# Attention heads loaded from GpSimd's queue, swaps and row sums ahead on SyncE's, the middle query tile in a slot of its own

## The chip, the cores and the metric

The kernel runs on one core of a Trainium2 chip. The metric is the device time of one execution in microseconds; the median of three runs of the kernel before is 1230.19 us (1230.02 to 1231.67). TensorE (PE) does the matmuls and transposes, VectorE (DVE), ScalarE (ACT) and GpSimd (POOL) the rest, and SyncE (SP) issues transfers. Times are in us from the start of the span.

## The reference: pooled attention, then two feed-forward stages

```python
q_pool = q.reshape(B, H, S // 2, 2, D).mean(axis=3)      # B, H, S, D = 2, 8, 1152, 64
scores = (1 / sqrt(D)) * matmul(q_pool, k^T)
attn = exp(scores - max); attn = attn / (sum(attn) + 1e-9)
x = matmul(attn, v)                                      # -> 1152 tokens x 512
h = x @ w_in; x = (h * tanh(softplus(h))) @ w_out        # 512 -> 2048 -> 512
P = sinkhorn(x @ w_gate)                                 # 8 rounds, 8 experts
out = sum over e of P[:, e] * (relu(x @ w1[e]) @ w2[e])  # 512 -> 1024 -> 512
```

All inputs are float32. The change touches the attention alone, which fills about the first 267 us of the span.

## The kernel before

**Tiles.** A batch has 8 heads, taken two at a time: 8 pairs p. A head has 576 pooled queries, so a pair has 1152, in nine tiles t of 128. Tiles 0 to 3 are the first head's, 5 to 8 the second's, and the middle tile (MID = 4) holds 64 queries of each. Every float32 operand is split into a high and a low part that sit side by side in the contracted dimension (2 x 64 = 128 rows). A step g = 9p + t handles one tile: scores of tile g (L451, into the one score buffer `ps_s`), a copy with the row maximum by VectorE (L466), the exponential by ScalarE (L480), a copy of the result `e` by DMA to a buffer `er` (`hand_over`, L482; two buffers), and, three steps behind, the transposes of `er` (L529), their split (L546, L549) and up to nine matmuls with v (`run_av`, L599).

**Preparation of the heads.** `split_kv` (L355) splits keys or values in two GpSimd operations, part 0 the high and part 1 the low one; `split_q` (L370) takes four steps: sum of the two pooled rows, scale, high, low. `PREP` (L618) gives the tile t at which each is put on GpSimd: `k10` and `k11` are the two parts of the second head's keys of the next pair. `kraw`, `vraw` and `qraw` have one buffer each, so the next load must wait for the last split of the one before. The loads (`load_kv` L333, `load_q` L340) are not issued where the split stands: they are put into the list `loads`, which the main loop empties onto SyncE's queue at the start of the next step (L703). A q load is four DMAs: one per head and one per half of the middle tile.

**Turning.** `trans_k` (L393) transposes keys on TensorE in three parts, `trans_q` (L436) four query tiles at once (u = 0: tiles 0 to 3, u = 1: 4 to 7, u = 2: tile 8), and ScalarE copies them to `qT`. Scores need the high and low rows also with their places exchanged: `swap` (L431), two DMAs from `qT` to itself, again through `loads`. The middle tile gets zero-padded operands `qz` (`middle`, L410) and a swap of its own. `TURN` (L623) gives the tile at which each stands.

**Row sums.** The sums of the exponentials of pair p are inverted and transposed (`turn_sums`, L493), written to DRAM (`out`) and read back, spread over partitions (`back`, three DMAs), both through `loads`; GpSimd multiplies the pair's output with them and splits it (`split_x`, L586). `wgs`, `raw`, `wt`, `wuh`, `wul` belong to weights that are prepared beside the attention.

All transfers of the kernel before are issued by SyncE. A step of the main loop puts its work in this order (shortened):

```python
pre = turn(p, t) if g < NQ else []
waiting, loads[:] = loads[:], []
for f in waiting: f()                 # SyncE: loads, swaps, row sums
scores(g); prep(p, t)                 # prep: GpSimd's splits
if pre: pre.pop(0)()                  # first turning of the step
transposes(g - LAG); hand_over(g - 1) # LAG = 3; hand_over: SyncE
run_av(min(ready, 9))
for f in pre: f()
exps(g)
```

An instruction that has to wait on an engine's queue holds back everything behind it on that queue.

Of the kernel before, what the change touches and what calls it, by code (L numbers as in the profile page):

```python
# [23 lines left out]
def pool_attention_mish_sinkhorn_kernel(  # L24
# [266 lines left out]
    with ExitStack() as actx:  # L291
# [34 lines left out]
        raws, kst, vst, kT, qst, qT = {}, {}, {}, {}, {}, {}  # L326
        loads = []

# [4 lines left out]
        def load_kv(p, j, which, t=None):  # L333
            b, hp, h0 = heads(p)
            t = t or kv_p.tile([P, NK, D], F32, tag=which + "raw", name=f"{which}raw{p}_{j}")
            src = (k if which == "k" else v)[b, h0 + j]
            nc.sync.dma_start(out=t, in_=src.rearrange("(p c) d -> p c d", c=NK))
            raws[which, p, j] = t

        def load_q(p, part=slice(0, QTL)):  # L340
            b, hp, h0 = heads(p)
            if part.start == 0:
                raws["q", p] = q_p.tile([P, QTL, 2, D], F32, tag="qraw", name=f"qraw{p}")
            for j in range(2):
                t0 = j * (MID + 1)
                ts = slice(max(part.start, t0), min(part.stop, t0 + MID))
                if ts.start < ts.stop:
                    src = q[b, h0 + j, 0:2 * MID * P].rearrange("(p t r) d -> p t r d", t=MID, r=2)
                    nc.sync.dma_start(out=raws["q", p][:, ts], in_=src[:, ts.start - t0:ts.stop - t0])
                if part.start <= MID < part.stop:  # L350
                    nc.sync.dma_start(
                        out=raws["q", p][j * D:(j + 1) * D, MID],
                        in_=q[b, h0 + j, 2 * MID * P:S].rearrange("(p r) d -> p r d", r=2))

        def split_kv(p, j, which, eng, part, more=True):  # L355
# [7 lines left out]
            else:  # L363
# [3 lines left out]
                if more and p < NPAIR:  # L367
                    loads.append(lambda: load_kv(p, j, which))

        def split_q(p, eng, step, part=slice(0, QTL)):  # L370
# [17 lines left out]
            if step == 3:  # L388
                split_lo(eng, qst[p][:, part, 1, :], qs, qst[p][:, part, 0, :])
                if part.stop == QTL and p + 1 < NPAIR:  # L390
                    loads.append(lambda: load_q(p + 1))

# [9 lines left out]

        def q_tile(p, t):
            u, i = divmod(t, 4)
            if (p, u) not in qT:
                n = min(4, QTL - 4 * u)
                qT[p, u] = qt_p.tile([P, 2, n, P], F32R, tag=f"qT{n}", name=f"qT{p}_{u}", bufs=2)
            return qT[p, u], i
# [8 lines left out]
        def trans_q0(u):  # L417

            n = min(2, QTL - 2 * u)
            ps = ps_t.tile([P, 2, 2, P], F32R, tag="t", name=f"psq0_{u}")  # L420
            for i in range(n):
                for s in range(2):
                    nc.tensor.transpose(
                        ps[:, i, s, :], qst[0][:, 2 * u + i, s:s + 2, :].rearrange("p a d -> p (a d)"), identr)
            t, i = q_tile(0, 2 * u)
            nc.scalar.activation(
                t[:, :, i:i + n].rearrange("p s n q -> p n s q"), ps[:, 0:n].bitcast(F32), AF.Copy)
            if 2 * u <= MID < 2 * u + n:
                middle(0, ps[:, MID - 2 * u], 2)

# [5 lines left out]
        def trans_q(p, u):  # L436
            ps = ps_t.tile([P, 4, P], F32R, tag="t", name=f"psq{p}_{u}")
            t, _ = q_tile(p, 4 * u)
            n = min(4, QTL - 4 * u)
            for i in range(n):  # L440
                nc.tensor.transpose(
                    ps[:, i, :], qst[p][:, 4 * u + i, 0:2, :].rearrange("p a d -> p (a d)"), identr)
            nc.scalar.activation(t[:, 0], ps[:, 0:n].bitcast(F32), AF.Copy)
            loads.append(lambda: swap(t))
            if 4 * u == MID:
                middle(p, ps, 1)
                loads.append(lambda: swap(qz[p % 2]))

        scS, eS, erS, rsS, rxS = {}, {}, {}, {}, {}

        def scores(g, pl=None):  # L451
            p, t = divmod(g, QTL)
            ps = (pl or ps_s).tile([P, 3, 512], F32, tag="s", name=f"psS{g}")
            for kb in range(3):
                if t == MID:
                    ops = [(qz[p % 2][:, s, j, :], kT[p, j]) for j in range(2) for s in range(2)]
                else:
                    x, i = q_tile(p, t)
                    ops = [(x[:, s, i, :], kT[p, int(t > MID)]) for s in range(2)]
# [33 lines left out]
        def turn_sums(p):  # L493
# [8 lines left out]
            def out():  # L502
                nc.sync.dma_start(out=row, in_=rt)
                loads.append(back)

# [5 lines left out]

            loads.append(out if p == NPAIR - 1 else lambda: loads.append(out))

# [97 lines left out]
        for m in range(1, 2 * NG1 - 1):  # L611
# [6 lines left out]
        PREP = {  # L618
            "q0": 1, "q1": 2, "q2": 3, "q3": 4, "v00": 1, "v01": 2, "v10": 5, "v11": 6,
            "k00": 2, "k01": 3, "k10": 7, "k11": 8,  # L620
        }
        PREP0 = {"k00": 3, "k01": 3, "q0": 4, "q1": 4, "q2": 5, "q3": 5, "v10": 5, "v11": 7, "k10": 7, "k11": 8}
        TURN = {"k0": (5, 6, 7), "k1": (0, 2, 3), "k10": (0, 0, 2), "q0": (2, 2, 3), "q": (6, 1, 2)}  # L623

# [45 lines left out]
        for part in range(4):  # L670
            split_q(0, nc.gpsimd, part, q2)
        def prep(p, t):
            for x, at_ in (PREP if p else PREP0).items():
# [22 lines left out]
        for g in range(T0 + EARLY):  # L696
# [5 lines left out]
            pre = turn(p, t) if g < NQ else []  # L702
            waiting, loads[:] = loads[:], []  # L703
            for f in waiting:
# [607 lines left out]
```

## Time and profile before

| | us |
|---|---|
| median of three runs (lowest, highest) | 1230.19 (1230.02, 1231.67) |
| the profiled execution | 1231.02 |
| its span on the core | 1229.0 |
| TensorE busy, share of the span | 1204.5, 98% |
| VectorE, ScalarE, GpSimd busy | 856.7, 593.8, 623.2 |

The profile is one execution. The span runs from the first to the last record on the core; the execution's own time is 2.0 us longer, for what lies around it. Busy time is the time in which an engine had an instruction in hand; instructions that only issue a DMA aren't counted. A row that says `A <- B` gives a wait of A and what ended it: for TensorE in the attention these are the rows to look for, since its idle time there is the time that a change can win.

### The profile page before, as it was taken

Reading aid. Unit: us, or ns where it says so; the run is one execution under the profiler, and the core shown is the slowest. Engines: PE = TensorE matmul, PEld = TensorE weight load, DVE = VectorE, ACT = ScalarE, POOL = GpSimd, SP = SyncE. Lnnn points to the kernel's source line nnn. Section 1 sums busy time; section 2 is a strip of 40 time slices with the busy share of each in tenths; the row PEclk is TensorE's granted clock in tenths of the full one; section 3 lists DMA queues with packets and bytes.
Section 4 is the critical chain, followed back from the end, with each engine's and each line's share of the span. In section 5 each row is a group of like instructions: output and inputs, shape, how many; then the busy total and the mean of one; then the engine's idle time right before and its main releaser. Section 6 shows DMA issues by size and latency. Waiting matters only on the chain.

```text
span 1229.0 us, 19413 instructions
## 1 busy us (share of the span) xinstructions
PE 1204.5 (98%) x6840; PEld 1113.0 (91%) x6840; DVE 856.7 (70%) x1596; ACT 593.8 (48%) x1364; POOL 623.2 (51%) x704
## 2 busy tenths in 40 slices
PE   8999999999999999999999999999999999999998
PEld 8998888999999999898888889999888899999887
DVE  7898888976444333787866777766866777866865
ACT  7888888977554443552333233333332333333331
POOL 5455566326434332384655565555555565555551
PEclk9999999999999999999999999999999999999999
DMA  6887777653323210011011111111112111111112
GB/s 199 276 277 256 259 251 274 229 192 115 91 69 90 82 31 31 1 52 48 25 40 52 52 43 53 52 52 41 33 39 52 52 43 52 53 52 37 37 39 77
DMA packets 56352, 116.85 MB, mean 95 GB/s; under 512 B 8312, under 2 KB 24896, under 8 KB 56256
## 3 DMA queue, kind: packets, MB, share of 16 engines
q1 hardware_dynamic: 56256, 115.62, 29.3%
q8 instruction: 54, 0.88, 0.3%
q14 instruction: 42, 0.34, 0.1%
HBM read 66.86 MB, written 2.40 MB: 56 GB/s over the span
## 4 chain that ended last, share of the span: by engine, by line
PE 90%; DMA 4%; DVE 3%; ACT 1%; issue 1%; POOL 0%; ACTq 0%; DVEq 0%; POOLq 0%; SPq 0%
PE po L1215 30%; PE c L1045 26%; PE ph L224 10%; PE po L784 8%; PE psS L461 5%; PE psA L564 4%; DMA er<-e 3%; PE psT L543 3%; DVE e L466 2%; DMA qT<-qT 1%; DVE etl L549 1%; PE psk L398 1%; ACT eth L546 0%; ACT e L480 0%; PE psw L629 0%
## 5 line engine op out<-in xcount | busy, mean ns | idle before, releaser
L81 POOL TENSOR_TENSOR wslotsl<-s,wslotsh 128x256 fp32r<-128x256 f32 x180 | 132.4, 744 | 239.2 <-ACT wslotsh L74 239.2
L1223 DVE SCALAR_TENSOR_TENSOR oacc<-po,Pm,oacc 128x512 f32<-128x512 f32 (+1 forms) x217 | 161.2, 747 | 102.9 <-PE po L1215 95.4
L1215 PE MATMUL po<-wdbl,hhall 128*128 128x512 f32 (+1 forms) x543 | 214.4, 395 | 0.0
L1215 PE MATMUL po<-wdbh,hlall 128*128 128x512 f32 (+1 forms) x543 | 214.1, 394 | 0.0
L1215 PE MATMUL po<-wdbh,hhall 128*128 128x512 f32 (+1 forms) x543 | 214.0, 394 | 0.0
L1062 ACT ACTIVATE t<-c 128x384 f32<-128x384 f32 x80 | 39.1, 489 | 248.2 <-PE c L1045 248.2
L1082 ACT ACTIVATE hhall<-c 128x384 fp32r<-128x384 f32 x180 | 88.6, 492 | 128.8 <-DVE c L1078 126.2
L1215 PEld LDWEIGHTS po<-wdbh,hhall 128*128 128x128 f32 x543 | 102.0, 188 | 24.4
L1215 PEld LDWEIGHTS po<-wdbl,hhall 128*128 128x128 f32 x543 | 102.0, 188 | 23.3
L1215 PEld LDWEIGHTS po<-wdbh,hlall 128*128 128x128 f32 x543 | 102.0, 188 | 23.3
L81 POOL TENSOR_TENSOR wslotsl<-rawu,wslotsh 128x256 fp32r<-128x256 f32 x120 | 90.7, 771 | 51.2 <-ACT wslotsh L74 51.2
L466 DVE TENSOR_SCALAR_CACHE_REDUCE e<-psS 128x1152 f32<-128x1152 f32 x72 | 97.3, 1352 | 23.8 <-DMA er<-e 10.5
L549 DVE TENSOR_TENSOR etl<-psT,eth 128x384 fp32r<-128x384 f32 (+1 forms) x240 | 108.0, 507 | 6.2 <-ACT eth L546 6.0
L1083 DVE SCALAR_TENSOR_TENSOR hlall<-c,hhall 128x384 fp32r<-128x384 f32 x180 | 98.7, 549 | 2.1
L546 ACT ACTIVATE eth<-psT 128x384 fp32r<-128x384 f32 (+1 forms) x240 | 92.4, 476 | 9.4 <-PE psT L543 9.1
L1045 PE MATMUL c<-x2h,wslotsl 128*128 128x384 f32 x280 | 94.7, 338 | 0.0
L461 PE MATMUL psS<-kT,qT 128*128 128x384 f32 x384 | 82.5, 347 | 12.5 <-DMA qT<-qT 6.4
L1045 PE MATMUL c<-x2h,wslotsh 128*128 128x384 f32 x280 | 94.4, 337 | 0.0
L1045 PE MATMUL c<-x2l,wslotsh 128*128 128x384 f32 x280 | 94.1, 336 | 0.0
L480 ACT ACTIVATE e<-e,nm 128x1152 f32<-128x1152 f32 x70 | 89.4, 1277 | 0.0
L74 ACT ACTIVATE wslotsh<-s 128x256 fp32r<-128x256 f32 x180 | 72.1, 411 | 24.3 <-DVE s L1011 24.3
L564 PE MATMUL psA<-etl,vst 128*128 128x256 f32 (+1 forms) x288 | 80.4, 303 | 0.5 <-DVE rs L490 0.5
(358 smaller groups left out, 3051.7 us busy)
## 6 DMA issues: line engine op xcount, KB each, us to landing
er<-e SPq DMA_DIRECT2D x70, 576.0 KB, 3.7
rawd<-in_moe_w_dram SPq DMA_DIRECT2D x60, 256.0 KB, 2.9
rawu<-in_moe_w_dram SPq DMA_DIRECT2D x30, 384.0 KB, 3.3
raw<-in_moe_w_in_dram SPq DMA_DIRECT2D x16, 512.0 KB, 4.1
raw<-in_moe_w_out_dram SPq DMA_DIRECT2D x16, 512.0 KB, 3.6
vraw<-in_v_dram SPq DMA_DIRECT2D x16, 288.0 KB, 3.2
kraw<-in_k_dram SPq DMA_DIRECT2D x15, 288.0 KB, 4.3
qraw<-in_q_dram SPq DMA_DIRECT2D x15, 256.0 KB, 6.2
```

The costliest lines, as they stand in the source:

```text
L81: eng.tensor_tensor(out=lo, in0=src, in1=hi.bitcast(F32), op=ALU.subtract)
L224: nc.tensor.matmul(ps[:, 0:TH], lhsT=a, rhs=b, start=(n == 0), stop=(n == len(ops) - 1))
L461: nc.tensor.matmul(ps[:, kb, 0:TH], lhsT=a, rhs=kt[:, kb * TH:(kb + 1) * TH], start=(n == 0), stop=(n == len(ops) - 1))
L466: nc.vector.tensor_scalar(sc, ps[:, :, 0:TH], -1.0, None, op0=ALU.mult, op1=ALU.min, accum_out=nm)
L546: nc.scalar.activation(eh[:, cs, o:o + b - a], ps[:, 0:3, a:b], AF.Copy)
L549: nc.vector.tensor_tensor(out=el[:, cs, o:o + b - a], in0=ps[:, 0:3, a:b], in1=eh[:, cs, o:o + b - a].bitcast(F32), op=ALU.subtract)
L564: nc.tensor.matmul(box["ps"][:, 0:n], lhsT=vst[p, j][:, c].rearrange("p a d -> p (a d)"), rhs=(el, eh)[which][:, c, 0:n], start=(c == 0 an ...
L784: nc.tensor.matmul(ps[:, 0:TH], lhsT=a, rhs=b, start=(n == 0), stop=(n == len(ops) - 1))
L1045: nc.tensor.matmul(cb[c], lhsT=a_, rhs=b_, start=FIRST[n] and m == 0, stop=LAST[n] and m == len(ops) - 1, skip_group_check=True)
L1083: los.append(lambda: nc.vector.scalar_tensor_tensor(out=lo, in0=b, scalar=0.0, in1=hi.bitcast(F32), op0=ALU.max, op1=ALU.subtract))
L1215: nc.tensor.matmul(ps[:, 0:w], lhsT=a, rhs=b[:, cs], start=(n == 0), stop=(n == len(ops) - 1))
L1223: nc.vector.scalar_tensor_tensor(out=oa, in0=ps[:, 0:w], scalar=gate, in1=oa, op0=ALU.mult, op1=ALU.add)
```

## The change

Loads of keys, values and queries of the main loop are issued on GpSimd's queue, right where the last split of their buffer stands, in place of SyncE's queue one step later (`loader`). Those of the start, before the main loop, stay on SyncE. A q load is one DMA for both heads and two for the middle tile. Swaps and row sums go into a list `first`, which is emptied ahead of `loads`; the row sums' `out` no longer waits a step more. In `qst` and `qraw` the middle tile takes the last slot (8), and tiles 5 to 8 take slots 4 to 7, so `qT` is two groups of four tiles, the middle tile is turned alone (u = 2) at t = 0 of its pair where u = 2 stood at t = 2, and the swap of a one-tile group is gone. `v11` moves from t = 6 to t = 5.

```diff
--- before.py
+++ after.py
@@ -324,7 +324,8 @@
             qz.append(t)
 
         raws, kst, vst, kT, qst, qT = {}, {}, {}, {}, {}, {}
-        loads = []
+        loader = nc.sync
+        loads, first = [], []
 
         def heads(p):
             b, hp = divmod(p, HPB)
@@ -334,22 +335,24 @@
             b, hp, h0 = heads(p)
             t = t or kv_p.tile([P, NK, D], F32, tag=which + "raw", name=f"{which}raw{p}_{j}")
             src = (k if which == "k" else v)[b, h0 + j]
-            nc.sync.dma_start(out=t, in_=src.rearrange("(p c) d -> p c d", c=NK))
+            loader.dma_start(out=t, in_=src.rearrange("(p c) d -> p c d", c=NK))
             raws[which, p, j] = t
 
         def load_q(p, part=slice(0, QTL)):
             b, hp, h0 = heads(p)
             if part.start == 0:
                 raws["q", p] = q_p.tile([P, QTL, 2, D], F32, tag="qraw", name=f"qraw{p}")
-            for j in range(2):
-                t0 = j * (MID + 1)
-                ts = slice(max(part.start, t0), min(part.stop, t0 + MID))
-                if ts.start < ts.stop:
-                    src = q[b, h0 + j, 0:2 * MID * P].rearrange("(p t r) d -> p t r d", t=MID, r=2)
-                    nc.sync.dma_start(out=raws["q", p][:, ts], in_=src[:, ts.start - t0:ts.stop - t0])
-                if part.start <= MID < part.stop:
-                    nc.sync.dma_start(
-                        out=raws["q", p][j * D:(j + 1) * D, MID],
+            src = q[b, h0:h0 + 2, 0:2 * MID * P].rearrange("h (p t r) d -> p h t (r d)", t=MID, r=2)
+            dst = raws["q", p][:, 0:2 * MID].rearrange("p (h t) r d -> p h t (r d)", h=2)
+            if part.stop - part.start == QTL:
+                loader.dma_start(out=dst, in_=src)
+            else:
+                h, ts = (0, part) if part.stop <= MID else (1, slice(0, MID))
+                loader.dma_start(out=dst[:, h, ts], in_=src[:, h, ts])
+            if part.stop == QTL:
+                for j in range(2):
+                    loader.dma_start(
+                        out=raws["q", p][j * D:(j + 1) * D, 2 * MID],
                         in_=q[b, h0 + j, 2 * MID * P:S].rearrange("(p r) d -> p r d", r=2))
 
         def split_kv(p, j, which, eng, part, more=True):
@@ -365,7 +368,7 @@
                 split_lo(eng, t[:, :, 1, :], raw, t[:, :, 0, :])
                 p, j = (p, 1) if j == 0 else (p + 1, 0)
                 if more and p < NPAIR:
-                    loads.append(lambda: load_kv(p, j, which))
+                    load_kv(p, j, which)
 
         def split_q(p, eng, step, part=slice(0, QTL)):
             if p == NPAIR:
@@ -388,7 +391,7 @@
             if step == 3:
                 split_lo(eng, qst[p][:, part, 1, :], qs, qst[p][:, part, 0, :])
                 if part.stop == QTL and p + 1 < NPAIR:
-                    loads.append(lambda: load_q(p + 1))
+                    load_q(p + 1)
 
         def trans_k(p, j, c3):
             if c3 == 0:
@@ -400,11 +403,14 @@
                 kT[p, j][:, c3 * TH:(c3 + 1) * TH],
                 ps[:, 0:3, :].bitcast(F32).rearrange("p a d -> p (a d)"), AF.Copy)
 
-        def q_tile(p, t):
-            u, i = divmod(t, 4)
+        def slot(t):
+
+            return t if t < MID else t - 1 if t > MID else 2 * MID
+
+        def q_tile(p, x):
+            u, i = divmod(x, MID)
             if (p, u) not in qT:
-                n = min(4, QTL - 4 * u)
-                qT[p, u] = qt_p.tile([P, 2, n, P], F32R, tag=f"qT{n}", name=f"qT{p}_{u}", bufs=2)
+                qT[p, u] = qt_p.tile([P, 2, MID, P], F32R, tag="qT", name=f"qT{p}_{u}", bufs=2)
             return qT[p, u], i
 
         def middle(p, ps, n):
@@ -422,11 +428,12 @@
                 for s in range(2):
                     nc.tensor.transpose(
                         ps[:, i, s, :], qst[0][:, 2 * u + i, s:s + 2, :].rearrange("p a d -> p (a d)"), identr)
+            if 2 * u == 2 * MID:
+                middle(0, ps[:, 0], 2)
+                return
             t, i = q_tile(0, 2 * u)
             nc.scalar.activation(
                 t[:, :, i:i + n].rearrange("p s n q -> p n s q"), ps[:, 0:n].bitcast(F32), AF.Copy)
-            if 2 * u <= MID < 2 * u + n:
-                middle(0, ps[:, MID - 2 * u], 2)
 
         def swap(t):
 
@@ -435,16 +442,17 @@
 
         def trans_q(p, u):
             ps = ps_t.tile([P, 4, P], F32R, tag="t", name=f"psq{p}_{u}")
-            t, _ = q_tile(p, 4 * u)
-            n = min(4, QTL - 4 * u)
+            n = min(MID, QTL - MID * u)
             for i in range(n):
                 nc.tensor.transpose(
-                    ps[:, i, :], qst[p][:, 4 * u + i, 0:2, :].rearrange("p a d -> p (a d)"), identr)
-            nc.scalar.activation(t[:, 0], ps[:, 0:n].bitcast(F32), AF.Copy)
-            loads.append(lambda: swap(t))
-            if 4 * u == MID:
+                    ps[:, i, :], qst[p][:, MID * u + i, 0:2, :].rearrange("p a d -> p (a d)"), identr)
+            if u == 2:
                 middle(p, ps, 1)
-                loads.append(lambda: swap(qz[p % 2]))
+                t = qz[p % 2]
+            else:
+                t, _ = q_tile(p, MID * u)
+                nc.scalar.activation(t[:, 0], ps[:, 0:n].bitcast(F32), AF.Copy)
+            first.append(lambda: swap(t))
 
         scS, eS, erS, rsS, rxS = {}, {}, {}, {}, {}
 
@@ -455,7 +463,7 @@
                 if t == MID:
                     ops = [(qz[p % 2][:, s, j, :], kT[p, j]) for j in range(2) for s in range(2)]
                 else:
-                    x, i = q_tile(p, t)
+                    x, i = q_tile(p, slot(t))
                     ops = [(x[:, s, i, :], kT[p, int(t > MID)]) for s in range(2)]
                 for n, (a, kt) in enumerate(ops):
                     nc.tensor.matmul(
@@ -501,7 +509,7 @@
 
             def out():
                 nc.sync.dma_start(out=row, in_=rt)
-                loads.append(back)
+                first.append(back)
 
             def back():
                 flat = row.rearrange("t p -> (t p)")
@@ -509,7 +517,7 @@
                     nc.sync.dma_start(
                         out=rx[j * D:(j + 1) * D, x:x + n], in_=flat[a:a + n].unsqueeze(0).to_broadcast([D, n]))
 
-            loads.append(out if p == NPAIR - 1 else lambda: loads.append(out))
+            first.append(out)
 
 
         c0, c1 = 2 * P, SQ
@@ -616,11 +624,11 @@
 
 
         PREP = {
-            "q0": 1, "q1": 2, "q2": 3, "q3": 4, "v00": 1, "v01": 2, "v10": 5, "v11": 6,
-            "k00": 2, "k01": 3, "k10": 7, "k11": 8,
+            "q0": 1, "q1": 2, "q2": 3, "q3": 4, "v00": 1, "v01": 2, "k00": 2, "k01": 3,
+            "v10": 5, "v11": 5, "k10": 7, "k11": 8,
         }
         PREP0 = {"k00": 3, "k01": 3, "q0": 4, "q1": 4, "q2": 5, "q3": 5, "v10": 5, "v11": 7, "k10": 7, "k11": 8}
-        TURN = {"k0": (5, 6, 7), "k1": (0, 2, 3), "k10": (0, 0, 2), "q0": (2, 2, 3), "q": (6, 1, 2)}
+        TURN = {"k0": (5, 6, 7), "k1": (0, 2, 3), "k10": (0, 0, 2), "q0": (2, 2, 3), "q": (6, 1, 0)}
 
 
 
@@ -669,6 +677,8 @@
         scores(1, ps_b)
         for part in range(4):
             split_q(0, nc.gpsimd, part, q2)
+        loader = nc.gpsimd
+
         def prep(p, t):
             for x, at_ in (PREP if p else PREP0).items():
                 if at_ == t:
@@ -700,7 +710,8 @@
                 ps_t = pool("ps_t", 4, space=PSUM)
                 ps_a = pool("ps_a", 1, space=PSUM)
             pre = turn(p, t) if g < NQ else []
-            waiting, loads[:] = loads[:], []
+            waiting = first + loads
+            first[:], loads[:] = [], []
             for f in waiting:
                 f()
             if g < LAG:
```

## Rows read from the trace of the kernel before

**Rows 1.** Busy time by stretch: us, then PE, PEld, DVE, ACT, POOL busy (instructions), PEclk, DMA share, GB/s
```profile
99.60:132.00 32.40, 30.41 (x241) 29.42 (x242) 29.28 (x60) 28.08 (x64) 19.11 (x20) 1.00 0.77 266
...
264.00:400.00 136.00, 135.86 (x788) 135.79 (x789) 65.58 (x121) 78.22 (x155) 57.49 (x44) 1.00 0.34 98
400.00:1229.00 829.00, 823.38 (x4145) 741.65 (x4144) 559.99 (x999) 288.12 (x698) 427.31 (x517) 1.00 0.15 45
...
48.00:232.00 184.00, 170.75 (x1347) 164.17 (x1345) 163.17 (x333) 159.51 (x360) 105.94 (x102) 1.00 0.77 263
```

**Rows 2.** Waits of PE, 48 to 232 us: total us, times, longest us
```profile
PE psS L461 <- DMA qT<-qT: 6.4, 6, 1.9
PE psT L543 <- DMA er<-e: 3.4, 6, 1.3
PE psS L461 <- DVE e L466: 2.9, 6, 0.5
```

**Rows 3.** Timeline of pair 3: start us, us, engine, line, operation, tiles [idle before <- releaser]
```profile
118.48 0.42 DVE L581 TENSOR_TENSOR xs<-psA,avt 64x256 f32<-64x256 f32 x1
...
124.36 0.60 ACT L443 ACTIVATE qT<-psq 128x512 fp32r<-128x512 f32 x1
...
125.90 0.92 PE L543 MATMUL psT<-identr,er 128*128 128x128 f32 x9 [0.42 <-DMA er<-e]
...
127.31 1.32 PE L461 MATMUL psS<-kT,qT 128*128 128x384 f32 x6 [0.48 <-DVE e L466]
...
132.02 1.12 PE L461 MATMUL psS<-kT,qT 128*128 128x384 f32 x5 [1.10 <-DMA qT<-qT]
...
132.97 0.37 PE L398 MATMUL psk<-identr,kst 128*128 128x128 f32 x3
```

**Rows 4.** SyncE's queue in pair 3, same columns (us: while the issues held the queue)
```profile
113.70 2.15 SPq L509 DMA_DIRECT2D rx<-row  x3
...
117.17 0.54 SPq L349 DMA_DIRECT2D qraw<-in_q_dram  x1
...
119.40 0.51 SPq L351 DMA_DIRECT2D qraw<-in_q_dram  x1
120.01 3.27 SPq L486 DMA_DIRECT2D er<-e  x2
127.06 0.33 SPq L337 DMA_DIRECT2D vraw<-in_v_dram  x1
127.44 1.12 SPq L434 DMA_DIRECT2D qT<-qT  x2
```

**Rows 5.** Waits of SyncE's queue, 0 to 268 us: total us, times, longest us
```profile
SPq L337 <- POOL vst L81: 20.6, 7, 3.8
```

**Rows 6.** Chain of work that ended last, pair 3: start us, us, what
```profile
120.01 5.76 DMA er<-e
127.98 3.91 DMA qT<-qT
```

**Rows 7.** DMA to landing: that of `er`, 30 to 265 us; key loads of the whole span (count, KB, us)
```profile
DMA to landing us min/median/max: 3.0/3.7/5.8
...
kraw<-in_k_dram SPq DMA_DIRECT2D x15, 288.0 KB, 4.3
```

**Rows 8.** Issue of key loads on SyncE's queue, 30 to 265 us: ns min/median/max
```profile
L337 SPq DMA_DIRECT2D kraw<-in_k_dram x12: 334/530/702, 33.3 to 215.4; - x12
```

**Rows 9.** GpSimd in pair 3, columns as in rows 3
```profile
110.49 0.68 POOL L78 TENSOR_SCALAR qst<-qraw 128x576 fp32r<-128x576 f32 x1 [6.81 <-PE psq L441]
...
112.53 1.44 POOL L81 TENSOR_TENSOR qst<-qraw,qst 128x576 fp32r<-128x576 f32 x1
120.01 1.44 POOL L590 TENSOR_TENSOR xs<-xs,rx 128x576 f32<-128x576 f32 x1 [6.04 <-DMA rx<-row]
...
130.09 1.44 POOL L81 TENSOR_TENSOR kst<-kraw,kst 128x576 fp32r<-128x576 f32 x1
```

**Rows 10.** ScalarE and PE in pair 0, columns as in rows 3
```profile
15.81 0.45 ACT L414 ACTIVATE qz<-psq 128x128 fp32r<-128x128 f32 x2
...
16.87 1.31 ACT L546 ACTIVATE eth<-psT 128x384 fp32r<-128x384 f32 x3
...
17.11 2.35 PE L461 MATMUL psS<-kT,qz 128*128 128x384 f32 x12
```

## The prediction

> **What bounds the kernel now.** The busy time by stretch comes first. After the attention TensorE has no gap that a change here could use: 135.86 of 136 us, then 823.38 of 829 us [rows 1]. In the attention it has. From 48 to 232 us, pairs 1 to 6, it is busy 170.75 of 184.0 us, so 13.2 us are idle; VectorE with 163.2 and ScalarE with 159.5 us stand close behind, GpSimd with 105.9 does not [rows 1].
>
> The waits of TensorE name that time: 6.4 us for `qT<-qT`, the swaps; 3.4 us for `er<-e`, the copies handed over; 2.9 us for VectorE's copy `e` [rows 2]. Together 12.7 of the 13.2 us. The third follows from the second: `e` writes a buffer that a late `er` copy has to read first.
>
> The timeline of pair 3 shows one period. TensorE waits 0.42 us for `er` at 125.90, 0.48 us for `e` at 127.31, 1.10 us for the swap at 132.02: 2.0 us in 32.4 [rows 3, 1].
>
> SyncE's queue shows why. ScalarE has written `qT` at 124.36 + 0.60 = 124.96 [rows 3], but its swap is issued at 127.44, behind a value load at 127.06 [rows 4]. That load waits for GpSimd's split of its buffer; such waits held the queue for 20.6 us in seven cases, up to 3.8 us [rows 5]. The swap's chain then ends 3.91 us after 127.98, at 131.89 [rows 6]. For `er` it is the q load: its DMAs go out from 117.17, the last at 119.40, the `er` copy at 120.01 behind them [rows 4], and that copy takes 5.76 us where the median is 3.7 [rows 6, 7].
>
> **The change, part by part.**
>
> *Loads off SyncE's queue.* Per full pair SyncE loses 4 issues for keys and values and 4 for q, with all waits for GpSimd's splits. The swap can then go out at about 125.0 in place of 127.44, and land 2.4 us earlier, at 129.5. TensorE stood ready for it at 132.02 - 1.10 = 130.92, and will at 130.0 when the 0.9 us of the two earlier waits are gone. Margin 0.5 us, so the 6.4 us go. The `er` copy no longer follows a q load: issued about as before, it needs its usual 3.7 us and not 5.76, so 2.1 us more are at hand than the 0.42 us that lacked. Then the 3.4 and, with them, the 2.9 us go. Sum of waits removed: 12.7 us.
>
> *Loads on GpSimd's queue.* Pairs 1 to 5 get seven issues each: two of keys, two of values, three of q; pairs 0 and 6 get some of them. No row shows an issue on GpSimd. Lower bound: SyncE's shortest issue of a key load, 0.33 us [rows 8]. Upper bound: an issue that held GpSimd until the data landed, 4.3 us [rows 7]. I take 1.0 us, between SyncE's median of 0.53 us for this same load [rows 8] and GpSimd's own two-input operation on a tile of that size, 1.44 us [rows 9]: the same work, done by that engine. [...]
>
> GpSimd's share: 19.1 us busy per pair [rows 1] + 7 x 1.0 = 26.1 in some 31, so it isn't the bound as a whole. But one stretch is tight. It starts with `xs` (the product with the row sums) at 120.01 and ends with `k11`, at 130.09 + 1.44 = 131.53 [rows 9]: 11.5 us with no gap. `k11` feeds `psk` of the next pair's t = 0, at 132.97 [rows 3], where TensorE would now be 2.0 us earlier, at 130.97. `xs` waited for `rx` (6.04 us idle [rows 9]). The change writes the row sums one step (32.4 / 9 = 3.6 us) earlier, so `rx`, issued at 113.70 [rows 4], lands near 116.4 in place of 120.0 and no longer sets it: VectorE's last piece of `xs`, ready at 118.48 + 0.42 = 118.90 [rows 3], does. So `xs` starts at 119.0, and `k11` ends at 119.0 + 11.5 + 1.0 for the v load now in the stretch = 131.5. TensorE waits 0.5 us. Pairs 2, 3 and 4 hold the same weight work there; pair 5 lacks one 0.7 us operation and comes out even. Price: 3 x 0.5 = 1.5 us. At 0.33 us an issue it is 0, at 4.3 us it is 3.8 us a pair and more.
>
> Behind `k11` on GpSimd stand the next load and the next pair's q steps; these have room. In the kernel before, the high part of q waits 6.81 us for `psq` of u = 2 [rows 9]; now the last group is u = 1, one step earlier, and the loads of k and q that follow go out earlier too. If that cover fails, `xs` starts later and `k11` with it, one for one.
>
> *Middle tile.* One swap (two issues) and one ScalarE copy less per pair; the two `qz` copies move from t = 1 to t = 0, four steps ahead of use. In pair 0 the middle tile is turned at t = 3, one step ahead of use. Its two copies (0.45 us [rows 10]) come in front of the first `eth` copies, as before, since the first turning of a step precedes the transposes. The `eth` of that step began at 16.87 and the scores on `qz` at 17.11 [rows 10]. I cost it at 0, between -0.3 (a copy less) and +0.45 us. The early `v11` precedes `k11` either way: 0.
>
> *What is late next.* Loads now leave in a burst behind GpSimd's splits and still pass through the same DMA engines, which are 77% busy [rows 1]; VectorE, with 163.2 us of work against 170.75 of TensorE's, leaves little room to catch up. I put back 0.42 us per pair, pair 3's wait for `er` [rows 3], for six pairs: 2.5 us. Bounds: 0, and 6.3 us where both `er` terms stay whole.
>
> **Sum.** 12.7 - 1.5 - 2.5 = 8.7 us off. The profiled execution's own 1231.0 becomes 1222.3; it lies 0.8 us above the median of the runs, so I forecast 1221.5. Behind the attention nothing swallows the gain: TensorE is full there, and the weights' loads are tied to the same steps, so they move along.
>
> [...] The `er` copy took 5.76 us right behind a q load and 3.7 in the median [rows 6, 7], while one queue carried both. [...]
>
> **The rivals.**
>
> 1. *The copies are as late as before*, since q loads and `er` share the engines. For it: the 77%. Against it: loads move to other moments, ahead of t = 4. The swaps' 6.4 us are won, the 6.3 us of `er` and `e` are not, and `k11` costs its 1.5: 4.9 us, 1225.3. Chance 0.15.
> 2. *All waits go and an issue on GpSimd is cheap* (0.33 us): 12.7 us, 1217.5. Chance 0.15.
> 3. *GpSimd becomes the bound* (slower). Its work per pair is 19.1 + 7c, with c the cost of an issue; the period is 32.4. It decides from c = (32.4 - 19.1) / 7 = 1.9 us. At 2.2 us the pair takes 34.5, 2.1 us more, over five pairs 10.5 us: 1240.7. [...] Against it: 2.2 us is four times SyncE's median issue. Chance 0.15.
> 4. *Even*: at about 1.9 us per issue gain and loss cancel, 1230. Chance 0.09.
>
> That the loads stay where they are isn't a rival: they are plain calls on another queue, and SyncE keeps only weights, swaps, row sums and `er`.
>
> **How the numbers follow.** Forecast 0.46, rivals 0.15, 0.15, 0.15 and 0.09. A difference of 0.2% (2.5 us) is about what a measurement of this kernel can tell from no change. Faster by over 0.2%: 0.46 + 0.15 + 0.15 = 0.76; within: 0.09; slower: 0.15. The low end, 1216.5, is rival 2 less 1 us for ScalarE's lighter load. The high end, 1234, takes in rivals 1 and 4 and the start of rival 3 (c = 2.0 gives 0.7 us a pair, 3.5 in all); what lies above, 0.14, and below, 0.05, is left out.
>
> **What would show it.** Right: `PE psS <- DMA qT` gone from the waits of TensorE, `er` and `e` below 2.5 us in all; swaps on SyncE within 0.2 us of ScalarE's `qT`; a new wait `PE psk <- POOL kst` of about 0.5 us in pairs 2 to 4; a pair near 31.3 us (32.4 - 2.0 + 0.5 + 0.4). Wrong: gaps of 2 us or more on GpSimd around its DMA issues, a period above 32.4 us with `psk` waiting for `kst`; or waits for `er` of the old size; or waits for weights after 264 us that give the gain back.

## The result, and the profile after

The changed kernel takes 1242.78 us in the median (1239.69 to 1242.97, four runs) against 1230.18 of the kernel before on the same chip (four runs): ratio 1.0092, 95% interval 1.0076 to 1.0108. The medians are 12.6 us apart, and the spans of the two profiled executions 11.5 us. The forecast of 1221.5 us, faster, was wrong in sign. The profiled execution took 1242.97 us, its span is 1240.5.

The four largest waits of TensorE from 48 to 232 us in the kernel after (total us, times, longest us), which answer to [rows 2]:

```profile
PE psq L447 <- DVE etl L557: 7.4, 4, 1.9
PE psS L469 <- DVE e L474: 5.9, 9, 0.9
PE psr L504 <- DVE rs L499: 1.4, 3, 0.5
PE psk L401 <- POOL kst L81: 1.2, 3, 0.4
```

Neither `qT` nor `er` stands there any more. The DMA waits of [rows 2] are gone, and VectorE has taken their place. From the timeline of pair 3 in the kernel after, VectorE, GpSimd and TensorE around t = 0 (start us, us, engine, line, operation):

```profile
95.97 1.36 DVE L474 TENSOR_SCALAR_CACHE_REDUCE e<-psS 128x1152 f32<-128x1152 f32 x1
96.56 0.60 POOL L338 DMA_DIRECT2D kraw<-in_k_dram  x1 [0.30 <-POOL kst L81]
97.18 1.43 POOL L379 TENSOR_TENSOR qraw<-qraw 128x576 f32<-128x576 f32 x1
97.25 4.17 DVE L156 TENSOR_SCALAR wt<-raw 128x256 uint32<-128x256 uint32 x1
98.57 0.68 POOL L78 TENSOR_SCALAR vst<-vraw 128x576 fp32r<-128x576 f32 x1
99.22 0.68 POOL L381 TENSOR_SCALAR qraw<-qraw 128x576 f32<-128x576 f32 x1
99.85 1.40 POOL L81 TENSOR_TENSOR vst<-vraw,vst 128x576 fp32r<-128x576 f32 x1
101.34 1.48 DVE L557 TENSOR_TENSOR etl<-psT,eth 128x384 fp32r<-128x384 f32 x3
101.55 0.58 POOL L338 DMA_DIRECT2D vraw<-in_v_dram  x1 [0.30 <-POOL vst L81]
101.94 0.53 PE L447 MATMUL psq<-identr,qst 128*128 128x128 f32 x4 [1.85 <-DVE etl L557]
102.17 0.69 POOL L78 TENSOR_SCALAR kst<-kraw 128x576 fp32r<-128x576 f32 x1
103.13 1.79 DVE L498 TENSOR_SCALAR rs<-rs 128x9 f32<-128x9 f32 x1
103.45 1.43 POOL L81 TENSOR_TENSOR kst<-kraw,kst 128x576 fp32r<-128x576 f32 x1
```

VectorE's shift of a weight piece (L156) begins at 97.25, just after GpSimd began a run of four splits with no gap between them. It ends at 101.42, right behind the end of the last one, 99.85 + 1.40 = 101.25, and ahead of the next DMA issue. The same happens to the add on nine row sums (L498): it ends at 104.92, behind the split that ends at 103.45 + 1.43 = 104.88. Behind L156 wait `etl`, and for `etl` TensorE, 1.85 us.

The same place of pair 3 in the kernel before:

```profile
101.29 1.45 POOL L81 TENSOR_TENSOR vst<-vraw,vst 128x576 fp32r<-128x576 f32 x1
102.21 0.68 DVE L156 TENSOR_SCALAR wt<-raw 128x256 uint32<-128x256 uint32 x1
103.00 0.68 POOL L78 TENSOR_SCALAR kst<-kraw 128x576 fp32r<-128x576 f32 x1 [0.27 <-DMA kraw<-in_k_dram]
104.60 0.15 DVE L490 TENSOR_SCALAR rs<-rs 128x9 f32<-128x9 f32 x1
```

There L156 starts 0.53 us before GpSimd's splits come to a pause (101.29 + 1.45 = 102.74) and ends 0.15 us behind that, and the add on the row sums stands while GpSimd is idle.

VectorE's groups from 60 to 250 us, kept apart by shape (xcount | busy us, mean ns | idle before). Kernel before:

```profile
L162 DVE SCALAR_TENSOR_TENSOR wt<-raw,wt 128x256 uint32<-128x256 uint32 x12 | 9.7, 809 | 0.0
L156 DVE TENSOR_SCALAR wt<-raw 128x256 uint32<-128x256 uint32 x12 | 5.8, 485 | 0.0
L490 DVE TENSOR_SCALAR rs<-rs 128x9 f32<-128x9 f32 x6 | 0.9, 153 | 0.0
```

Kernel after, the same operations:

```profile
L156 DVE TENSOR_SCALAR wt<-raw 128x256 uint32<-128x256 uint32 x12 | 20.0, 1670 | 0.0
L498 DVE TENSOR_SCALAR rs<-rs 128x9 f32<-128x9 f32 x6 | 7.8, 1296 | 0.0
L162 DVE SCALAR_TENSOR_TENSOR wt<-raw,wt 128x256 uint32<-128x256 uint32 x11 | 7.6, 691 | 0.0
```

The work is the same, but for one L162 that falls behind 250 us in the kernel after, and takes 35.4 us in place of 16.4. L162 is not part of the rise: its mean is 809 ns before and 691 after. The other part of the loss is TensorE's clock. Busy time of 2 us windows in the kernel after (PE, PEld, DVE, ACT, POOL; then PEclk, DMA share, GB/s):

```profile
106.00:108.00 2.00, 1.32 (x6) 1.00 (x6) 2.00 (x5) 1.35 (x2) 1.70 (x2) 1.00 0.93 272
108.00:110.00 2.00, 1.97 (x13) 1.83 (x14) 2.00 (x4) 1.34 (x3) 1.29 (x3) 0.56 0.55 54
110.00:112.00 2.00, 2.00 (x9) 2.00 (x10) 1.97 (x6) 0.49 (x2) 0.00 (x0) 0.59 1.02 384
112.00:114.00 2.00, 2.00 (x20) 1.96 (x19) 1.24 (x3) 1.71 (x4) 0.00 (x0) 1.00 0.42 165
```

Between 100 and 108 us TensorE was busy for 0.15, 2.00, 1.11 and 1.32 us of the four windows of 2 us, at a granted clock of 1.00. Behind that the granted clock is 0.56 and 0.59 of full speed from 108 to 112 us, though TensorE is busy again. The same comes in pair 4 (0.50 at 146 us) and pair 6 (0.51 at 214 us, 0.50 at 216 us), not in pair 5 (1.00 from 182 to 186 us). Over the span TensorE is busy 1212.8 us against 1204.5 before, 8.3 us more for the same 6840 matmuls, and idle 27.7 against 24.5, 3.2 us more; together the 11.5 us by which the span grew. In wt_later below, with the stalls gone, the granted clock is 1.00 from 0 to 267 us, and TensorE's first 1956 matmuls take 252.05 us of busy time, as in the kernel before (252.16), against 260.4 in the kernel after.

Time between the starts of two score copies `e` on VectorE's timeline, pair 3 (us; the last step runs to the next pair's t = 0):

| kernel | t = 0 to 1 | 1 to 4 | 4 to 8 | 8 to 0 | pair |
|---|---|---|---|---|---|
| before | 3.99 | 10.77 | 13.07 | 4.66 | 32.49 |
| after | 9.11 | 12.38 | 12.96 | 2.77 | 37.22 |
| best2 | 4.24 | 11.22 | 16.82 | 2.90 | 35.18 |
| gap | 3.61 | 11.14 | 18.31 | 3.16 | 36.22 |
| q_on_sync | 4.17 | 11.23 | 13.59 | 2.78 | 31.77 |

The rows are of the profiled executions. That of q_on_sync, 1223.8 us, is close to its median, but best2's took 1230.64 and gap's 1242.58 us, 4.4 and 6.1 us above theirs. The gain forecast is there where the swap's wait was, from t = 8 to 0. It is lost, more than twice over, in the step behind it.

### The profile page after: what moved, and what is told of

Read it like the earlier page. It is cut to its first block, busy times and chain, and to the rows that moved or that the text cites. A ratio compares the mean times of both kernels' runs of the same rounds, so it can differ in the third digit from the quotient of the medians.

```text
span 1240.5 us, 19363 instructions
## 1 busy us (share of the span) xinstructions
PE 1212.8 (98%) x6840; PEld 1117.6 (90%) x6840; DVE 875.2 (71%) x1596; ACT 593.2 (48%) x1356; POOL 651.4 (53%) x750
## 4 chain that ended last, share of the span: by engine, by line
PE 90%; DVE 7%; issue 2%; ACT 1%; POOL 0%; ACTq 0%; POOLq 0%; DVEq 0%
PE po L1226 30%; PE c L1056 25%; PE ph L224 10%; PE po L795 8%; PE psS L469 5%; PE psA L572 5%; PE psT L551 3%; DVE etl L557 2%; DVE e L474 2%; DVE wt L156 1%; PE psk L401 1%; DVE rs L498 1%; PE psw L637 0%; PE pg L850 0%; DVE wt L162 0%
```

## The experiments

The theory (H in the texts on record): a run of GpSimd's splits without a gap holds VectorE's operations that read and write SBUF alone until it ends, and the change makes these operations start early in such runs. Its rivals put the loss on the transfers that GpSimd issues, or on VectorE as a full engine.

### The held operations moved: wt_later, sums_in_psum, both

wt_later moves the four weight operations of VectorE, which stood at t = 0 to 3, to t = 3 and 4:

```diff
-                at(ts[1] + 2 * j, "dve", lambda cs=cs: shift(cs))
-                at(ts[1] + 2 * j + parts - 1, "dve", lambda cs=cs: sign(cs))
+                w = ts[1] + j if parts > 1 else ts[1]
+                at(w, "dve", lambda cs=cs: shift(cs))
+                at(w, "dve", lambda cs=cs: sign(cs))
...
-        load_w(0, 0, [(t, t + 2, t + 7, t + 8, t + 9) for t in evenly(16, 9)], 2, parts=2, busy=True)
+        load_w(0, 0, [(t, t + 5, t + 7, t + 8, t + 9) for t in evenly(16, 9)], 2, parts=2, busy=True)
...
```

The next line, for the second weight, changes alike. sums_in_psum leaves the weights and does the row sums' add and reciprocal behind their transpose, on PSUM; both has the two edits.

```diff
-            nc.vector.tensor_scalar(rs, rs, EPS, None, op0=ALU.add)
-            nc.vector.reciprocal(rs, rs)
...
-            nc.vector.tensor_copy(rt, ps[0:QTL, 0, :])
+            nc.vector.tensor_scalar(ps[0:QTL, 0, :], ps[0:QTL, 0, :], EPS, None, op0=ALU.add)
+            nc.vector.reciprocal(rt, ps[0:QTL, 0, :])
```

> Theory H (held): a VectorE operation with all its operands in SBUF gets no start while GpSimd runs without a gap. In the changed kernel the weight operations of VectorE (wt, L156) stood 1.67 us in the mean where 0.28 us is their least, 16.6 us too much over 60 to 250 us. Here they move to t = 3 and t = 4 of a pair, where GpSimd stands idle behind its loads. H expects wt at 0.28 us again, most of 16 us back: 1226 to 1231 us, while rs still stands 1.8 us. Theory G (GpSimd is the bound, by its seven DMA issues of 0.6 to 0.7 us and a 0.3 us wait each): nothing moves by more than 2 us, 1241 to 1244 us.

> Only the row sums' two small VectorE operations change: they are done behind the transpose, with PSUM as their source, and no longer on the SBUF tile rs (1.30 us in the mean where 0.15 is the least, 6.9 us too much over six pairs). H expects the new operations at 0.3 us or less each, and 4 to 8 us back: 1235 to 1239 us, with wt still held for about 4 us. G: no change, 1241 to 1244 us.

> Both moves in one kernel. H: VectorE is free of holds, the waits that the change removed stay removed, TensorE's clock has no reason to fall: 1217 to 1222 us, below the kernel before. G: 1240 us or more.

Measured: wt_later 1227.59 us (ratio 0.9977, 0.9966 to 0.9989): the whole loss and 2.6 us more come back, though every load is still issued on GpSimd, and L156 takes 290 ns in the mean. sums_in_psum 1239.46 (1.0071, 1.0056 to 1.0086) is 0.5 us above its range. both 1227.4 (0.9974, 0.996 to 0.9988) is 5.4 us above its range and no better than wt_later. The replacement is dear itself: VectorE's groups of L156 in wt_later and of the new reciprocal in both, 946 ns for nine rows:

```profile
L156 DVE TENSOR_SCALAR wt<-raw 128x256 uint32<-128x256 uint32 x12 | 3.5, 290 | 0.0
...
L506 DVE RECIPROCAL rt<-psr 9x128 f32<-9x128 f32 x6 | 5.7, 946 | 0.2
```

So the weight operations carry most of the loss.

### One held operation put back: best, probe_add, probe_reciprocal

best is wt_later with the add of the row sums on ScalarE. The probes add to it one useless operation of nine elements at t = 0, its result unused:

```diff
...
-            nc.vector.tensor_scalar(rs, rs, EPS, None, op0=ALU.add)
+            nc.scalar.activation(rs, rs, AF.Copy, bias=EPS)
...
+                if p and t == 0 and g < NQ:
+                    nc.vector.tensor_scalar(probe, ones[:, 0:9], 1.0, None, op0=ALU.add)
```

In probe_reciprocal the last line is `nc.vector.reciprocal(probe, ones[:, 0:9])`.

> The changed kernel with VectorE's weight operations at t = 3 and t = 4, and the 1e-9 added to the row sums by ScalarE; the reciprocal stays on VectorE, since it took 0.215 us in every run, held or not. H: rs is gone from the held operations, the step t = 0 to t = 1 shrinks from 5.5 us (weights moved alone) to about 4.1, with the next step at 2.85: 1.4 us in each of four to five pairs less than the 1227.6 of the weights moved alone: 1220 to 1224 us. Rival S (what is left is set by VectorE's own work and TensorE, and the hold of rs lies beside other work): 1226 to 1229 us.

> As the kernel called best, with one useless VectorE operation in step t = 0 of each pair from 1 to 7, behind the copy of the scores: 9 elements per partition, SBUF to SBUF, an add. Its result is not used. H: it is held until GpSimd's run has its next gap, 2 to 4 us in pairs 2 to 5, and the kernel gets slower than best by 6 us or more. Rival (VectorE's long weight operations were slow by their own size, 256 elements with a stride of two): 0.06 to 0.2 us an operation and at most 1 us in all.

> The same useless operation at the same place and of the same size, but a reciprocal. If every SBUF operation of VectorE is held by GpSimd's run, it stands 2 to 4 us too and the time is that of probe_add. If only some forms are held, as the steady 0.215 us of the reciprocal behind rs suggests, it stands 0.22 us and the kernel is within 2 us of best.

best 1227.88 (0.9976, 0.9963 to 0.999) missed its 1220 to 1224 and came out in its rival's range; VectorE now waits for ScalarE's add, 7.1 us in six times. probe_add 1236.41 (1.0056, 1.0035 to 1.0078), probe_reciprocal 1230.05 (0.9996, 0.9984 to 1.0008). VectorE's group of the probe in probe_add, and the probe of pair 3 in the timeline beside GpSimd's last split of that run:

```profile
L734 DVE TENSOR_SCALAR probe<-ones 128x9 f32<-128x9 f32 x6 | 12.1, 2016 | 0.0
...
100.87 4.07 DVE L734 TENSOR_SCALAR probe<-ones 128x9 f32<-128x9 f32 x1
103.50 1.40 POOL L82 TENSOR_TENSOR vst<-vraw,vst 128x576 fp32r<-128x576 f32 x1
```

The same group in probe_reciprocal:

```profile
L734 DVE RECIPROCAL probe<-ones 128x9 f32<-128x9 f32 x6 | 1.3, 209 | 0.0
```

An add of nine elements, 0.17 us in pairs 1, 2 and 7, takes 4.07 us until GpSimd's run ends at 104.90; in pairs 4 to 6 it takes 3.95, 1.24 and 2.50 us. The seven cost the kernel 8.5 us against best and 6.4 against probe_reciprocal. A reciprocal of the same size in the same place is not held: its seven took 0.21 us each, and its kernel is 2.2 us slower than best, close to the 2 us set. At the same size and place one kind is held and the other is not: that tells the theory from a VectorE that is merely full, and narrows it to some kinds of operation.

### Gaps opened in GpSimd's run: gap

The changed kernel, with two tiny GpSimd operations a pair that read VectorE's results, so that GpSimd stands still while VectorE works:

```diff
...
+                if parts == 2 and cs.start == 0:
+                    x = box["t"][:, 0:1].bitcast(I32)
+                    nc.gpsimd.tensor_tensor(out=mark_i, in0=x, in1=x, op=ALU.add)
...
+            if p < NPAIR - 1:
+                nc.gpsimd.tensor_scalar(mark_f, rs, 1.0, 0.0, op0=ALU.mult, op1=ALU.add)
```

> The changed kernel with every operation of VectorE where the change left it. Added are two tiny GpSimd operations per pair that read what VectorE wrote: one element per partition of wt behind the first weight operation of a chunk (t = 0), and the nine row sums behind their reciprocal. GpSimd must wait for VectorE there, so its run gets a gap exactly where VectorE needs one; it has 6 to 11 us to spare later in the pair. H: wt at t = 0 and rs fall to 0.3 and 0.15 us, the step t = 0 to t = 1 from 9.1 to about 4.5 us, 4 us or more in each of pairs 3 to 6: 1222 to 1229 us. If the operations are slow for their own place or size, or GpSimd's work is what bounds: 1240 us or more, since GpSimd only gets more to do.

1236.47 us (1.0048, 1.0029 to 1.0066), 7.5 us above its range and 3.5 below the rival's. The timeline of pair 3 shows that the hold itself is gone:

```profile
105.06 0.29 DVE L158 TENSOR_SCALAR wt<-raw 128x256 uint32<-128x256 uint32 x1
105.44 0.18 POOL L163 TENSOR_TENSOR mark_i<-wt 128x1 int32<-128x1 int32 x1 [4.42 <-DVE wt L158]
107.08 0.15 DVE L503 TENSOR_SCALAR rs<-rs 128x9 f32<-128x9 f32 x1
107.65 0.21 POOL L506 TENSOR_SCALAR mark_f<-rs 128x9 f32<-128x9 f32 x1 [2.02 <-DVE rs L504]
```

0.29 us in place of 4.17 (in all of pairs 2 to 6), and t = 0 to 1 takes 3.61 us in place of 9.11 (table above): the expected effect in its place. But GpSimd stands idle for 4.42 and 2.02 us, its next value load goes out 8.6 us behind the `e` copy of t = 0 in place of 5.6, and from t = 4 to 8 the pair loses 5 us. The waits of TensorE from 48 to 232 us name `er`; that the later loads make it late was not tried by itself:

```profile
PE psT L558 <- DMA er<-e: 13.8, 6, 3.2
```

### Where the loads are issued: loads_on_sync, before_moved, loads_alone, sync_moved

loads_on_sync puts all loads of the changed kernel back through the list (`loads.append(lambda: load_kv(p, j, which))`, the same for q); sync_moved has that and the moves of best2 below. loads_alone is the kernel before with nothing but its loads issued by GpSimd right behind their splits. before_moved is the kernel before with the moves of best.

> The changed kernel with its loads back on SyncE's queue, through the list as in the kernel before; the early middle tile, the order of swaps and row sums and the merged q load stay. G (the issues on GpSimd are what costs): back to 1230 us or below. H (GpSimd's gapless run holds VectorE, with or without DMA issues in it): rs and wt are still held for 1.5 us or more each, 1232 us or more.

> The kernel before with the same two moves and nothing of the change. In it wt stood 0.48 us and its second operation 0.81 us in the mean, together 7 us above their least over six pairs, partly under waits for DMA. H: 0 to 5 us faster than before, 1225 to 1230 us, with the waits for the swaps and for er whole: slower than best by 3 us or more. If best is no faster than this one, the change itself gives nothing.

> The kernel before with one part of the change alone: keys, values and queries loaded from GpSimd's queue behind its splits. Middle tile, swaps, row sums and v11 as before. H: the waits of TensorE for the swaps and er fall to 3 us or less, the pair's boundary comes earlier, so wt at t = 0 starts earlier in GpSimd's run and is held 3 to 4 us; rs falls into the gap in which GpSimd waits for the last query turning and stays at 0.15 us: 1231 to 1238 us, between the two kernels. If the loads were good by themselves and the middle tile did the harm: 1224 us or less.

> The changed kernel with loads back on SyncE and the same two moves as best2. It tells what GpSimd's queue is worth once nothing is held: the waits for er (8.5 us in loads_on_sync) should stay, the rest as in best2: 3 to 6 us slower than best2. If it is as fast, the loads' move is worth nothing by itself.

loads_on_sync took 1230.1 (1.0001, 0.9982 to 1.002), where the theory had wanted a loss and holds of 1.5 us or more. Its rival's time was right. What speaks against the rival is wt_later, which keeps every issue on GpSimd and takes 1227.59 us, and the timeline gives a cause that fits the theory:

```profile
99.15 1.44 POOL L81 TENSOR_TENSOR vst<-vraw,vst 128x576 fp32r<-128x576 f32 x1
100.06 0.68 DVE L156 TENSOR_SCALAR wt<-raw 128x256 uint32<-128x256 uint32 x1
100.99 0.67 POOL L78 TENSOR_SCALAR kst<-kraw 128x576 fp32r<-128x576 f32 x1 [0.40 <-DMA kraw<-in_k_dram]
```

GpSimd's run, with no issue in it, ends at 99.15 + 1.44 = 100.59. L156 starts 0.53 us before that end and ends 0.15 us behind it, at 100.74, in the 0.40 us wait for a load. What L156 paid was the rest of the run that it started in: 0.68 us with 0.53 us left here, 4.17 us with 4.0 us left in the changed kernel. before_moved 1230.77 (1.0005, 0.9995 to 1.0015) is 0.8 us above its range and 2.9 us above best: the moves by themselves win nothing in the kernel before. It isn't a kernel without holds, though. GpSimd is busy where L156 now stands: it takes 726 ns in the mean against 485, and the reciprocal waits 5.1 us for ScalarE.

loads_alone 1247.91 (1.0147, 1.0131 to 1.0163) was slower than either theory had it. From its chain of waits in pair 3 (start us, us, what):

```profile
122.91 8.53 DMA er<-e
131.44 0.14 issue
131.57 1.36 PE psT L544 x9
```

An `er` copy takes 8.53 us there, beside a q load that GpSimd issued from 121.39 to 123.57 and a weight load of 512 KB that SyncE issued at 119.25; TensorE waits 14.6 us for `er` in five times. On one queue the longest copy had taken 5.8 us [rows 7]. Which of the two loads makes the copy late isn't shown by this kernel. sync_moved 1232.51 (1.002, 1.0008 to 1.0032) is 6.3 us above best2, where 3 to 6 were set: with L156 at 0.29 us in both, all loads on GpSimd are worth that much against all on SyncE. Its wait for `er` is 4.7 us, not the 8.5 expected.

### What is left of the forecast: best2, q_on_sync, q_in_halves

best2 is wt_later with the add of the row sums on ScalarE at the end of t = 8, where nothing waits for it:

```diff
                 if g < NQ:
                     exps(g)
+                    if t == QTL - 1:
+                        nc.scalar.activation(rsS[p], rsS[p], AF.Copy, bias=EPS)
```

q_on_sync is best2 with the q load alone back on SyncE, one step later (`loads.append(lambda: load_q(p + 1))`, `nc.sync` in `load_q`). q_in_halves keeps it on GpSimd and issues the second head's half and the middle tile two steps later.

> As best, but ScalarE adds the 1e-9 at the end of t = 8, before the step in which VectorE takes the reciprocal; in best the reciprocal waited 1.2 us a pair for ScalarE, so the hold was only traded for a wait. H: the step t = 0 to t = 1 falls from 5.2 to 4.0 us in pairs 2 to 6, 5 to 6 us in all: 1220 to 1224 us. Rival S (VectorE and TensorE fill the pair anyway): 1226 to 1229 us.

> best2 with the q loads alone back on SyncE's queue, one step later and behind the swaps and row sums; keys and values stay on GpSimd. Theory C (what is missing of the gain is the er copy that lands late beside a q load): on SyncE the q load and the er copies go out one after the other, the waits psT <- er fall from 7.1 us to under 4, time 1222 to 1225. Rival V (VectorE has no room, the er waits only show where the slack ends): waits move to another name, 1225 to 1228. If the one queue is what made er late, as the prediction had it for the kernel before, er waits come back to 3.4 and more and the time is above 1226.

> best2 with the q load on GpSimd cut in two: the first head's half (256 KB) behind the last q split as now, the second half and the middle tile two steps later. Theory C: no er copy meets more than half of the load, psT <- er falls from 7.1 us to under 4, time 1222 to 1225. Rival V: 1225 to 1228, with er waits near 7 or under another name.

best2 1226.21 (0.9971, 0.9957 to 0.9985), 2 us above its range and in its rival's; q_on_sync 1224.19 (0.9952, 0.9935 to 0.9969), as theory C had it, the lowest median of all kernels here, though its interval overlaps best2's; q_in_halves 1233.46 (1.0026, 1.0012 to 1.0039), above both of its ranges. TensorE's waits from 48 to 232 us, best2:

```profile
PE psT L551 <- DMA er<-e: 7.1, 4, 2.4
PE psS L470 <- DVE e L475: 2.9, 6, 0.5
PE psk L402 <- POOL kst L81: 0.9, 2, 0.5
```

q_on_sync:

```profile
PE psS L470 <- DVE e L475: 2.9, 6, 0.5
PE psk L402 <- POOL kst L81: 1.2, 3, 0.4
```

q_in_halves:

```profile
PE psk L404 <- POOL kst L81: 6.4, 4, 1.8
PE psS L472 <- DVE e L477: 2.9, 6, 0.5
PE psT L553 <- DMA er<-e: 0.5, 2, 0.2
```

With the q load off GpSimd's queue the wait for `er` is gone; with half of it moved away it is nearly gone too, so in these traces it was the q load and not a lack of room on VectorE. But the moved half stands ahead of `k11` on GpSimd, and what `er` won `psk` loses. How much the q load costs is less sure: the 7.1 us are those of an execution of best2 that took 1230.64 us, the medians of best2 and q_on_sync are 2.0 us apart, and in best and both, with the q load in the same place, TensorE waits only 1.5 and 1.8 us for `er`. Nor do the waits explain the whole time of q_in_halves: they sum to 9.8 us against best2's 10.9, and its median is 7.3 us higher. That stays open.

## Why the prediction was wrong

**Swaps off the loads' queue: right.** ScalarE's `qT` of pair 3 ends at 126.14 + 0.60 = 126.74 and the swap is issued at 126.76; the 6.4 us of [rows 2] are gone. The swap of t = 1 goes out 0.9 us behind its `qT`, after an `er` copy, and TensorE doesn't wait for it.

**Row sums and `k11`: right.** GpSimd's `xs` waits for VectorE, no longer for `rx`, and `psk` waits 0.4 us at most in three pairs, 1.2 us in all (again in q_on_sync), where 1.5 was set.

**Issue on GpSimd: about right.** A k or v load holds it 0.59 us behind 0.30 us for its own split; a q load 0.30 + 0.73 + 1.05. Seven make 4 x 0.89 + 2.08 = 5.6 us a pair, 0.8 each against 1.0. Rival 3 had the sign and, with 1240.7, nearly the time, but by luck: 0.8 is far from the 2.2 us an issue that it needs for that, and GpSimd still waits 54.9 us for VectorE's `xs` from 48 to 248 us.

**The step that failed: VectorE's own operations.** The sum took every duration on VectorE as fixed and looked for GpSimd's effect only in what waits for GpSimd. The step "What is late next" named VectorE's lack of room and put at most 6.3 us on it. No term stood for a GpSimd run that holds VectorE, though the trace of before had it: L156 ran from 276 to 1401 ns there around a median of 288, L162 from 408 to 1445 around 422. The change moved VectorE against GpSimd. In the kernel before, L156 of pair 3 started 0.53 us before the run of splits ended and took 0.68 us; in the kernel after it starts 4.0 us before the end (97.25 against 101.25), with all four splits still to come, because the swap's wait ahead of it is gone and a k load, 0.30 + 0.60 us, now stands ahead of the four. The add of the row sums falls on splits that in [rows 9] stood behind the 6.81 us wait for `psq`; "go out earlier too" in the prediction was that wait's end, and only its use was costed. The price is what wt_later gives back by moving L156 and L162, 1242.78 - 1227.59 = 15.2 us, or 14 by the two ratios, clock included. The sum had no term for TensorE's clock either: 8.3 of the 11.5 us by which the span grew are longer busy time, and in wt_later, without the stalls, they are gone. None of the prediction's signs of being wrong names this: the period of pair 3 is above 32.4 us, but without long waits of `psk`.

**`er`: too hopeful.** "It needs its usual 3.7 us" failed for the copy that meets the q load: 7.14 us in best2's chain, 8.53 in that of loads_alone. 2.5 us were put back; best2's profiled execution waits 7.1 us for `er` and 2.9 for `e`, 10.0 in all, above the upper bound of 6.3; in best's they are 1.5 and 3.3 us, below it. In the changed kernel no wait for `er` shows, since its pairs were longer. With the holds gone, best2 comes out at 1226.21, 0.9 us from rival 1, which had left the `er` terms whole. These late copies and the q load beside them had different issuers, and they took longer than the 5.76 us of the copy right behind a q load on one queue [rows 6]. All loads on GpSimd's queue still gained against all on SyncE's: sync_moved is 6.3 us above best2.

**`e`: wrong.** Its 2.9 us were to go with `er`'s. In q_on_sync no `er` wait is left and `e` still costs 2.9 us in six times. One of the six, in pair 3, has this ahead of it:

```profile
122.93 1.36 DVE L475 TENSOR_SCALAR_CACHE_REDUCE e<-psS 128x1152 f32<-128x1152 f32 x1 [0.47 <-PE psS L470]
```

VectorE's copy waited 0.47 us for TensorE's scores, not for `er`, and the next scores, at 124.35, wait 0.47 us for the copy. Both use the one score buffer.

With the holds and the q load repaired, q_on_sync's profiled execution takes 1223.8 us, against the 1222.3 of the sum; its pair takes 31.8 us against 31.3. That it comes so near is in part luck: the 2.9 us of `e` that did not go and the 2.5 us put back for `er` that were not needed nearly cancel. By medians q_on_sync is 6.0 us below the kernel before, where the sum had 8.7 for the change.

## What to carry to other kernels

Before closing gaps on GpSimd, look at the shortest, median and longest duration of each VectorE operation that reads and writes SBUF alone: here a long tail whose end fell on a pause of GpSimd was a hold, and it grew with what was left of GpSimd's run (L156: 0.68 us with 0.53 us left, 4.17 us with 4.0 us left). Move such operations out of the run (290 ns in the mean in wt_later), or try a form that is not held (here a reciprocal, 0.21 us in the add's place). Then move loads one kind at a time; here the one that met a copy on the path did better behind it on the same queue, by 2.0 us between medians.

## What was not expected of the hardware

The hold: 4.17 us for a 0.29 us shift, 4.07 us for a 0.17 us add, over four GpSimd operations in a row. The two-input L162 was held too (423 ns in the median, 1172 at most, in the kernel after); a reciprocal never was (215 to 216 ns in the kernel after).

The kinds held here: L156 and the two adds (up to 4.20, 1.79 and 4.07 us) are `tensor_scalar`, and L162 (up to 1.17 us in the kernel after) has two inputs in SBUF. L156 of pair 3 stayed in hand over four instructions of GpSimd and ended 0.17 us behind the last, in GpSimd's first pause of 0.30 us. Which operations are held and until when is what the runs show; by what, none of them shows.

The clock: TensorE's granted clock stood at 1.00 up to the stalls of t = 0 in pair 3 and at 0.56 and 0.59 in the 2 us windows behind them, at 0.50 and 0.51 in windows of pairs 4 and 6, and at 1.00 throughout in pair 5, from 176 to 188 us; in pair 3 a `psA` matmul of 320 columns took 0.47 us there against 0.31 a step before. That the 8.3 us of added busy time are gone in wt_later fits the clock as their cause; whether a part of them has another was not tried.
